# A fused scan and feed-forward kernel: attention operands loaded ahead of the weights, sign rows made in one go, the order searched anew

## The chip, the core and the metric

The kernel runs on one core of a Trainium2 chip. The core has TensorE (PE, matrix multiplies, with weight loads shown apart as PEld), VectorE (DVE), ScalarE (ACT) and GpSimd (POOL), and SyncE (SP), whose queue issues every DMA of this kernel. [...] The metric is the device time of one execution in microseconds, as the median of several runs; less is better.

## The reference, cut to what matters

A chunked linear recurrence with decay produces an array of 3072 tokens by 256, and a feed-forward layer follows:

```
log_a = log(clip(a, 1e-6, 1))
for c in chunks:                          # the chunk length is free
    cum   = cumsum(log_a[chunk])
    M     = (C @ B.T) * exp(cum_i - cum_j) * (i >= j)
    y     = M @ x + (C @ state) * exp(cum_i)
    state = exp(cum_last) * state + sum_j exp(cum_last - cum_j) * outer(B_j, x_j)
h = y @ w_in                              # 3072 x 256 by 256 x 2048
g = h - tanh(h)
out = g @ w_out                           # 2048 x 256
```

There are 4 batches, 8 heads, 768 positions, 32 columns per head and 16 state rows per head. All is float32.

## The kernel before, in words

**Attention part.** Each batch is cut into 7 chunks of 112 positions (the last has 96). The 16 state rows sit as extra rows 0 to 15 beside the 112 positions, so one product per head gives both the inner and the carried part. For a chunk, TensorE makes decay differences (L447 for the first three chunks, L512 for the later ones) and the products of B and C (L458, L521) in the PSUM tile `att`; ScalarE takes the exponential (L465, L536) into `lt`; VectorE multiplies by the products (L470, L540); GpSimd zeroes what is not causal (L475, L543); TensorE makes `y` (L569, L575). ScalarE copies the new state from `y` into the rows of the next chunk's `x` (L580), and `y` is split into a high and a low part, `xh` by ScalarE (L593) and `xl` by VectorE (L598). So each chunk hands its state to the next, and the chunks of a batch form a chain.

**Decays.** `a` arrives in `a_sb`, is clipped on VectorE (`logs`, L804), and ScalarE takes the logarithm into `la` (L840), then loads the table for the exponential (L817). TensorE sums `la` (L863, L868); ScalarE takes the sums as `ncum` (L897) and `rows` (L873); VectorE splits the rows into three bfloat16 `parts` (L877 to L875); a DMA stores them (L882), and small DMAs read them back into rows of `lt_c` (L888) and `rt_c` (L890). L512 multiplies `lt_c` with `rt_c`: the rows that were read back are the sums, the other rows of a group of nine are ones or signs. The ones of `lt_c` come from a GpSimd memset (L827). The signs of `rt_c` are `lt_c` while it is still all ones, times the column `par` (L496): four instructions in two spans of chunks, and the loads into `lt_c` of a span wait for them.

**Feed-forward part.** Tokens are taken in 12 tiles of 256. The two halves of a 256-row piece of the weights come by DMA as `raw` and are split by `conv` (L348 to L372) into `wh` and `wl`. A step (tile, piece) is `mm1` (L646, 12 matmuls), `act` (tanh L661, difference L665, split L669 and L676) and `mm2` (L709, 12 matmuls). Steps (0,0) and (0,1) use unsplit operands (L630, L701).

**Order.** All work is listed as operations with an engine, a cost and dependencies (class `Order`). A table of numbers, `RANK`, gives each a priority; a list scheduler (`schedule`) with the written costs makes a plan, and the operations are issued in the order of that plan. SP allows itself eight transfers in flight. In gaps of TensorE that the plan shows in its first 65 us, `fill` (L434) puts in matmuls whose result is not used; `warm` (L834) does so at the start. The number of fills in a long gap depends on `LATE`.

Of the kernel before, what the change touches and what calls it, by code (L numbers as in the profile page):

```python
# [42 lines left out]
NPH, NL, NSW, NRAW, NGB, LAG, WARM = 2, 3, 4, 2, 3, 2, 8  # L43
SWEEPS = 0, 2, 4, 6, 8
AHEAD = 32
LULL, SPARE, PIECE, LATE = 65.0, 0.35, 0.215, 1.4
# [207 lines left out]
def tile_ssm_moe(ctx: ExitStack, tc: tile.TileContext, a, x, bn, bc, wts, out):  # L254
    nc = tc.nc
# [569 lines left out]
    def ones(i):  # L825
        v = lt_c[:, SPAN[i]].rearrange("p c m -> p (c m)")
        nc.gpsimd.memset(v, 1.0)  # L827
# [175 lines left out]
```

## Time and profile before

| | |
|---|---|
| median of three runs | 336.06 us (334.4 to 338.8) |
| profiled execution | 337.54 us, span 335.8 us |
| TensorE busy | 326.6 us (97%) |
| VectorE busy | 226.6 us (67%) |
| ScalarE busy | 192.0 us (57%) |
| GpSimd busy | 56.8 us (17%) |

The span is from the first to the last instruction that the profile records; 1.7 us of the profiled execution lie around it. Shares over the span are averages over stages with different limits: the first 42 us carry little feed-forward work, the rest carries most of it.

### The profile page before, as it was taken

To read this page: it belongs to the slowest core of one execution; us is meant where nothing else is said; L and a number is where in the kernel's file an instruction comes from. 1 tells how busy PE (TensorE), PEld (TensorE's weight loads), DVE (VectorE), ACT (ScalarE), POOL (GpSimd) and SP (SyncE) were. 2 spreads that over 40 slices of the span, in tenths; PEclk is the share of its full clock that TensorE was granted. 3 is DMA by queue.
4 is the path that set the end of the run, shared out by engine and by line. 5 is a ranking of instruction groups with operands and counts; after the bars stand their busy time and mean duration, and the time that the engine had idled before them with its cause. 6 is when DMAs were issued, how large, how long until landed. Compare 5 with 4: busy or idle time off the path is not lost.

```text
span 335.8 us, 9087 instructions
## 1 busy us (share of the span) xinstructions
PE 326.6 (97%) x3872; PEld 314.4 (94%) x3872; DVE 226.6 (67%) x332; ACT 192.0 (57%) x404; POOL 56.8 (17%) x74
## 2 busy tenths in 40 slices
PE   8899999999999999999999999999999999999995
PEld 6788789999999999999999999999999999999995
DVE  2779999999998975645555655655655655654552
ACT  5766888784775644344555645643656645644441
POOL 6543464610102110000011101101111101100000
PEclk9699999999999999999999999999999999999999
DMA  6939668640102102010011200200200100100000
GB/s 158 263 112 307 153 230 193 194 143 0 48 9 68 32 0 65 31 33 2 31 48 31 64 12 20 64 20 13 62 4 2 33 2 2 33 0 2 31 2 32
DMA packets 12472, 21.41 MB, mean 64 GB/s; under 512 B 2848, under 2 KB 7648, under 8 KB 12432
## 3 DMA queue, kind: packets, MB, share of 16 engines
q1 hardware_dynamic: 12432, 20.84, 21.9%
q8 instruction: 30, 0.49, 0.6%
q14 instruction: 10, 0.08, 0.1%
HBM read 17.51 MB, written 3.32 MB: 62 GB/s over the span
## 4 chain that ended last, share of the span: by engine, by line
PE 87%; DMA 4%; DVE 4%; issue 2%; ACT 1%; POOL 1%; SPq 1%; POOLq 0%
PE o L709 39%; PE ph L646 38%; PE y L569 4%; PE att L521 3%; DMA bc<-bc_d 3%; DMA raw<-w_d 2%; PE att L512 1%; PE cp L447 1%; PE y L575 1%; POOL lt L543 1%; DVE lt L470 1%; DVE wm L353 0%; DVE g L665 0%; PE att L458 0%; DVE rt_c L496 0%
## 5 line engine op out<-in xcount | busy, mean ns | idle before, releaser
L665 DVE TENSOR_TENSOR g<-ph,g 128x512 f32<-128x512 f32 x96 | 66.1, 690 | 55.9 <-ACT g L661 55.9
L661 ACT ACTIVATE g<-ph 128x512 f32<-128x512 f32 x96 | 57.5, 599 | 74.3 <-PE ph L646 71.7
L646 PE MATMUL ph<-xh,wh 128*128 128x256 f32 x376 | 95.3, 278 | 0.2 <-DVE g L665 0.2
L646 PE MATMUL ph<-xh,wl 128*128 128x256 f32 x376 | 94.5, 276 | 0.0
L676 DVE TENSOR_TENSOR gl<-g,gh 128x512 fp32r<-128x512 f32 x94 | 66.7, 713 | 26.6 <-ACT gh L669 24.0
L669 ACT CAST gh<-g 128x512 fp32r<-128x512 f32 x94 | 58.2, 619 | 36.0 <-DVE g L665 29.7
L646 PE MATMUL ph<-xl,wh 128*128 128x256 f32 x376 | 73.2, 276 | 0.0
L646 PEld LDWEIGHTS ph<-xh,wh 128*128 128x128 f32 x376 | 70.6, 188 | 0.8 <-DVE g L665 0.4
L646 PEld LDWEIGHTS ph<-xh,wl 128*128 128x128 f32 x376 | 70.6, 188 | 0.0
L709 PE MATMUL o<-gh,wh 128*128 128x256 f32 x376 | 60.2, 282 | 0.0
L709 PE MATMUL o<-gh,wl 128*128 128x256 f32 x376 | 57.9, 276 | 0.0
L709 PE MATMUL o<-gl,wh 128*128 128x256 f32 x376 | 57.9, 276 | 0.0
L646 PEld LDWEIGHTS ph<-xl,wh 128*128 128x128 f32 x376 | 56.6, 188 | 0.0
L709 PEld LDWEIGHTS o<-gh,wh 128*128 128x128 f32 x376 | 49.8, 188 | 1.1
L709 PEld LDWEIGHTS o<-gh,wl 128*128 128x128 f32 x376 | 49.6, 188 | 0.0
L709 PEld LDWEIGHTS o<-gl,wh 128*128 128x128 f32 x376 | 49.6, 188 | 0.0
L543 POOL TENSOR_SCALAR_AFFINE_SELECT lt<-lt 128x896 f32<-128x896 f32 (+1 forms) x25 | 28.6, 1143 | 122.3 <-DVE lt L540 109.5
L540 DVE TENSOR_TENSOR lt<-att,lt 128x896 f32<-128x896 f32 (+1 forms) x25 | 26.6, 1065 | 2.8 <-ACT lt L536 2.1
L396 POOL TENSOR_TENSOR bw<-braw,wdec 128x256 f32<-128x256 f32 x14 | 12.3, 886 | 90.7 <-PE y L575 89.9
L536 ACT ACTIVATE lt<-att 128x896 f32<-128x896 f32 (+1 forms) x25 | 22.6, 904 | 1.4 <-PE att L521 0.3
L580 ACT COPY x<-y 16x64 f32<-16x64 f32 x96 | 19.4, 202 | 6.4 <-DVE xl L598 3.5
L569 PE MATMUL y<-lt,x 128*32 128x112 f32 (+1 forms) x448 | 16.8, 268 | 1.9 <-POOL lt L543 1.2
(79 smaller groups left out, 264.1 us busy)
## 6 DMA issues: line engine op xcount, KB each, us to landing
raw<-w_d SPq DMA_DIRECT2D x16, 512.0 KB
x<-x_d SPq DMA_DIRECT2D x14, 256.0 KB
bc<-bc_d SPq DMA_DIRECT2D x56, 60.0 KB
out_d<-ob SPq DMA_DIRECT2D x16, 128.0 KB
braw<-bn_d SPq DMA_DIRECT2D x14, 112.0 KB
out_d<-pt SPq DMA_DIRECT2D x8, 128.0 KB
cum<-parts SPq DMA_DIRECT2D x1, 168.0 KB
lt_c<-cum SPq DMA_DIRECT2D x4, 27.0 KB
```

What stands on the lines that cost most here:

```text
L396: nc.gpsimd.tensor_tensor(out=d["b"].rearrange("p c (h n) -> p c h n", h=H), in0=d["braw"].rearrange("p c (h n) -> p c h n", h=H), in1=wd. ...
L536: nc.scalar.activation(k["l"][:, :, 0:q].rearrange("p (i w) q -> p i w q", i=4), place[1][:, :, 0:2, N : N + q], AF.Exp)
L540: nc.vector.tensor_tensor(out=lt, in0=place[1][:, :, 2:4, N : N + q], in1=lt, op=ALU.mult)
L543: nc.gpsimd.affine_select(out=k["l"][:, :, 0:q], in_=k["l"][:, :, 0:q], pattern=[[0, H], [1, q]], compare_op=ALU.is_ge, fill=0.0, base=N, ...
L569: nc.tensor.matmul(out=y[D * h : D * h + D, hg * Q : hg * Q + q], lhsT=d["x"][:, cg, P * hg + D * h : P * hg + D * h + D], rhs=k["l"][:, 4 ...
L580: nc.scalar.copy(grp[(ck + 1) // CPG]["x"][0:N, (ck + 1) % CPG, 2 * D * i : 2 * D * i + 2 * D], k["y"][D * i : D * i + N, H * D : H * D + ...
L646: nc.tensor.matmul(out=ph[:, j, :], lhsT=w_[:, u, 0, k, j * P : (j + 1) * P], rhs=d[("xh", "xl")[p]][:, k, ts], start=p == 0 and k == 0 an ...
L661: nc.scalar.activation(g, gs[t, u][0], AF.Tanh)
L665: nc.vector.tensor_tensor(out=g, in0=ph, in1=g, op=ALU.subtract)
L669: nc.scalar.copy(gh, gs[t, u][1])
L676: on.tensor_tensor(out=gl, in0=g, in1=gh.bitcast(F32), op=ALU.subtract)
L709: nc.tensor.matmul(out=po[t, seg][:, e, :], lhsT=w_[:, u, 1, j, e * P : (e + 1) * P], rhs=g[:, j, :], start=u == seg[0] and k == 0 and j = ...
```

## The change

The sign rows are made early and for all chunks at once: VectorE sets the 3200 columns of one half of `rt_c` to one, and two multiplications by the columns of `par` write the second half and then the first. The four multiplications of before (L496) are gone, and with them the wait of the loads into `lt_c`. `WARM` goes from 8 to 10 and `LATE` from 1.4 to 0.6. The planner counts a longer lag from a DMA to its reader. `RANK` is a new table.

```
-NPH, NL, NSW, NRAW, NGB, LAG, WARM = 2, 3, 4, 2, 3, 2, 8
+NPH, NL, NSW, NRAW, NGB, LAG, WARM = 2, 3, 4, 2, 3, 2, 10
...
-LULL, SPARE, PIECE, LATE = 65.0, 0.35, 0.215, 1.4
+LULL, SPARE, PIECE, LATE = 65.0, 0.35, 0.215, 0.6
...
-147 351 639 203 244 86 296 353 131 427 266 928 811 84 242 227 476 72 88 71 191 74 773 287 117 117 324 209 273 250 172
...
+128 962 150 26 11 291 361 128 296 162 1269 342 704 181 590 195 876 1242 131 302 195 963 256 1239 184 545 130 28 258
...
     def lag(self, a, b):
-        return self.DMA_LATENCY if a == "DMA" else 0.0 if a == b else self.SEM_PE if "PE" in (a, b) else self.SEM
+        if a == "DMA":
+            return {"POOL": 2.4, "DVE": 1.3, "ACT": 1.3}.get(b, self.DMA_LATENCY)
+        return 0.0 if a == b else self.SEM_PE if "PE" in (a, b) else self.SEM
...
                 s = ck // 2
                 sl = SPAN[s]
-                for w in range(2):
-                    op("DVE", (0.45, 0.8)[s], lambda w=w, sl=sl: nc.vector.tensor_scalar(
-                           out=rt_c[:, w, sl], in0=lt_c[:, sl], scalar1=par[:, w : w + 1], scalar2=None, op0=ALU.mult),
-                       r=[l_c[s], "par", k["n_l"][1]], w=[r_c[s]])
...
     r_c = op.pieces("rt_c", 2)
+    sign = [rt_c[:, w, SPAN[0].start :].rearrange("p c m -> p (c m)") for w in range(2)]
+    op("DVE", 0.9, lambda: nc.vector.memset(sign[0], 1.0), w=r_c)
+    for w in (1, 0):
+        op("DVE", 0.95, lambda w=w: nc.vector.tensor_scalar(out=sign[w], in0=sign[0], scalar1=par[:, w : w + 1], scalar2=None,
+                                                            op0=ALU.mult), r=["par"], w=r_c)
```

**VectorE at the start.** The first of the program's rows on VectorE, before (L804 is the clip of `a`, L807 to L813 make `par` and `idn`, L353 begins the first weights):

```order
L789 MEMSET a_sb 16x224
L790 MEMSET a_sb 32x32
L804 TENSOR_SCALAR a_sb<-a_sb 128x224
L807 TENSOR_SCALAR pid<-pid 128x1
L808 TENSOR_SCALAR pid<-pid 128x1
L809 CAST pidf<-pid 128x2
L810 CAST ncf<-ncol 128x16
L811 TENSOR_SCALAR par<-pidf 128x1
L812 TENSOR_SCALAR par<-pidf 128x1
L813 TENSOR_SCALAR idn<-ncf,pidf 128x16
L353 TENSOR_SCALAR wm_163<-raw_126 128x512
L358 TENSOR_SCALAR wv_170<-wv_170 128x512
```

and in the change (L848 and L850 are the new work, L805 is the clip):

```order
L790 MEMSET a_sb 16x224
L791 MEMSET a_sb 32x32
L848 MEMSET rt_c 128x3200
L808 TENSOR_SCALAR pid<-pid 128x1
L809 TENSOR_SCALAR pid<-pid 128x1
L810 CAST pidf<-pid 128x2
L811 CAST ncf<-ncol 128x16
L812 TENSOR_SCALAR par<-pidf 128x1
L813 TENSOR_SCALAR par<-pidf 128x1
L814 TENSOR_SCALAR idn<-ncf,pidf 128x16
L850 TENSOR_SCALAR rt_c<-rt_c,par 128x3200 x2
L805 TENSOR_SCALAR a_sb<-a_sb 128x224
```

The clip moved from third to last of these, behind the memset, the small constants and both sign multiplications; the first two weight instructions moved behind the split of the rows.

**VectorE in the first tile.** Before, around the sign multiplications of the second span (`lt` and `xl` belong to the first three chunks, `wl`, `wm`, `wv` to the first weights):

```order
L470 TENSOR_TENSOR lt_287<-att,lt_287 128x448
L353 TENSOR_SCALAR wm_377<-raw_223 128x1024
L372 TENSOR_TENSOR wl<-wv_170,wh 128x512
L496 TENSOR_SCALAR rt_c<-lt_c,par 128x2304
L598 TENSOR_TENSOR xl_320<-y_331,xh_311 128x2x112
L358 TENSOR_SCALAR wv_388<-wv_388 128x1024
L361 SCALAR_TENSOR_TENSOR wm_377<-wv_388,wm_377 128x1024
```

and the same place in the change:

```order
L475 TENSOR_TENSOR lt_287<-att,lt_287 128x448
L377 TENSOR_TENSOR wl<-wv_221,wh 128x512
L599 TENSOR_TENSOR xl_317<-y_333,xh_302 128x2x112
L358 TENSOR_SCALAR wm_382<-raw_246 128x1024
L377 TENSOR_TENSOR wl<-wv_221,wh 128x512
L363 TENSOR_SCALAR wv_406<-wv_406 128x1024
L366 SCALAR_TENSOR_TENSOR wm_382<-wv_406,wm_382 128x1024
```

The multiplication is gone, and `xl` of the second chunk stands ahead of one `wl` and of `wm`.

**SP at the start.** The first transfers before:

```order
L315 DMA braw_99<-bn_d 112x256
L792 DMA a_sb<-a_d 112x192
L794 DMA a_sb<-a_d 96x32
L325 DMA raw_126<-w_d 128x1024
L294 DMA bc_128<-bc_d 16x960 x4
L325 DMA raw_126<-w_d 128x1024
L306 DMA x_141<-x_d 128x512
L306 DMA x_144<-x_d 128x512
```

and in the change:

```order
L793 DMA a_sb<-a_d 112x192
L299 DMA bc_131<-bc_d 16x960
L795 DMA a_sb<-a_d 96x32
L311 DMA x_134<-x_d 128x512
L299 DMA bc_131<-bc_d 16x960
L311 DMA x_145<-x_d 128x512
L299 DMA bc_131<-bc_d 16x960 x2
L320 DMA braw_99<-bn_d 112x256
L330 DMA raw_153<-w_d 128x1024 x2
```

The attention operands `bc`, `x` and `braw` moved ahead of the first weights `raw`; the second piece of `a` keeps the third place.

## Rows read from the trace of the kernel before

**Rows 1.** The page's engine line: busy time, share of the span, instructions.

```profile
PE 326.6 (97%) x3872; PEld 314.4 (94%) x3872; DVE 226.6 (67%) x332; ACT 192.0 (57%) x404; POOL 56.8 (17%) x74
```

**Rows 2.** Busy time by stretch: stretch, its length, then PE, PEld, DVE, ACT, POOL busy with instructions, granted TensorE clock, DMA share, GB/s.

```profile
7.60:18.70 11.10, 9.02 (x109) 7.95 (x107) 7.07 (x15) 8.72 (x30) 4.28 (x6) 0.69 0.97 253
18.70:42.10 23.40, 21.54 (x344) 18.37 (x343) 22.90 (x30) 16.94 (x41) 10.95 (x12) 1.00 0.66 188
42.10:68.70 26.60, 26.37 (x435) 24.30 (x420) 26.33 (x34) 22.13 (x51) 14.32 (x14) 1.00 0.71 201
...
100.00:331.50 231.50, 231.50 (x2613) 227.31 (x2612) 138.08 (x204) 119.02 (x239) 19.52 (x25) 1.00 0.09 26
```

**Rows 3.** The timeline in order of time (start, duration, engine, line, what; in brackets the idle time before it and what ended it): the first feed-forward step with split weights, and the one later idle gap of TensorE.

```profile
42.14 0.38 PE L646 MATMUL ph<-xh,wh 128*128 128x256 f32 x1
...
68.70 0.38 PE L646 MATMUL ph<-xh,wh 128*128 128x256 f32 x1 [0.23 <-DVE g L665]
```

**Rows 4.** The timeline of the opening: clip, logarithm, tables, constants, and the first exponential.

```profile
1.20 0.09 DVE L790 MEMSET a_sb<- 32x32 f32 x1
...
3.60 0.28 DVE L804 TENSOR_SCALAR a_sb<-a_sb 128x224 f32<-128x224 f32 x1 [2.31 <-DMA a_sb<-a_d]
...
3.90 0.61 ACT L840 ACTIVATE la<-a_sb 128x224 f32<-128x224 f32 x1 [1.61 <-DVE a_sb L804]
3.94 0.15 DVE L807 TENSOR_SCALAR pid<-pid 128x1 int32<-128x1 int32 x1
...
4.53 1.28 ACT L817 ACT_TABLE_LOAD   x1
...
4.64 0.33 DVE L813 TENSOR_SCALAR idn<-ncf,pidf 128x16 f32<-128x16 f32 x1
...
5.83 0.20 ACT L817 ACTIVATE tab<-const-float32-1.0 128x1 f32<-128x1 f32 x1
...
7.60 0.68 ACT L348 ACTIVATE wv<-raw 128x512 f32<-128x512 f32 x1 [1.57 <-DMA raw<-w_d]
...
8.18 0.35 ACT L873 COPY rows<-pr 112x256 f32<-112x256 f32 x1
...
8.43 0.36 ACT L897 ACTIVATE ncum<-pr 128x224 f32<-128x224 f32 x1
8.65 0.29 DVE L877 CAST parts<-rows 112x256 bf16<-112x256 f32 x1
8.82 1.09 ACT L465 ACTIVATE lt<-cp,ncum 128x112 f32<-128x112 f32 x4
```

**Rows 5.** Groups of instructions in the first 90 us, shapes apart: busy time, mean ns of one, idle time before and its releaser.

```profile
L496 DVE TENSOR_SCALAR rt_c<-lt_c,par 128x2304 bf16<-128x2304 bf16 x2 | 2.1, 1066 | 0.0
L496 DVE TENSOR_SCALAR rt_c<-lt_c,par 128x896 bf16<-128x896 bf16 x2 | 1.1, 608 | 0.0
L353 DVE TENSOR_SCALAR wm<-raw 128x512 uint32<-128x512 uint32 x2 | 0.8, 424 | 2.6 <-DMA raw<-w_d 2.6
L358 DVE TENSOR_SCALAR wv<-wv 128x512 f32<-128x512 f32 x2 | 0.8, 422 | 0.3 <-ACT wv L348 0.3
L789 DVE MEMSET a_sb<- 16x224 f32 x1 | 0.2, 245 | 0.9 <-PEq L993 0.9
L827 POOL MEMSET lt_c<- 128x2304 bf16 x1 | 2.0, 2022 | 0.0
L470 DVE TENSOR_TENSOR lt<-att,lt 128x448 f32<-128x448 f32 x6 | 3.7, 622 | 3.6 <-ACT x L580 2.2 <-PE att L458 1.4
```

**Rows 6.** Busy time of VectorE alone in two stretches (length, busy time with instructions, granted clock, DMA share, GB/s); the second ends with the split of the fifth chunk.

```profile
8.65:18.70 10.05, 6.31 (x14) 0.66 0.98 254
18.70:40.90 22.20, 21.70 (x29) 1.00 0.66 189
```

**Rows 7.** The timeline of ScalarE's one long wait between the first exponentials.

```profile
14.31 0.62 ACT L369 CAST wh<-wv 128x512 fp32r<-128x512 f32 x1 [1.64 <-DVE wv L365]
```

**Rows 8.** TensorE's timeline: the warm-up, the sums and first differences, the idle gap, and the same differences later.

```profile
0.84 3.59 PE L834 MATMUL warm<-const-float32-1.0 128*32 128x128 f32 x16 [0.84 <-PEq L993]
...
4.66 0.66 PE L863 MATMUL pr<-upto,la 128*112 128x128 f32 x4 [0.23 <-POOL after L799]
...
5.54 1.04 PE L447 MATMUL cp<-upto,la 128*128 128x112 f32 x8
...
9.55 0.71 PE L458 MATMUL att<-bc 16*128 16x112 f32 x16 [1.70 <-POOL bc L403]
...
12.85 3.75 PE L447 MATMUL cp<-upto,la 128*128 128x112 f32 x16
```

**Rows 9.** The granted clock of TensorE by microsecond (stretch, length, PE busy, granted clock, DMA share, GB/s).

```profile
12.00:13.00 1.00, 1.00 (x17) 0.50 1.14 186
...
18.00:19.00 1.00, 1.00 (x20) 0.95 0.56 160
```

**Rows 10.** The chain of waits that ended last (start, length, what), where a sign multiplication stands on it.

```profile
24.31 1.11 DVE rt_c L496
```

**Rows 11.** SP's issues of the first weights and of the store of the parts in the timeline, and TensorE's first use of what is read back.

```profile
2.18 0.43 SPq L325 DMA_DIRECT2D raw<-w_d  x1
...
10.21 0.33 SPq L882 DMA_DIRECT2D cum<-parts  x1
...
27.03 0.27 PE L512 MATMUL att<-rt_c,lt_c 9*128 9x224 bf16 x4
```

97 rows, old and new, of the table RANK are left out of this document.

## The prediction

> **What bounds the kernel now.** The page's engine line comes first: TensorE is busy 97% of the span [rows 1]. Shares over the span hide stages, so the stretches come next [rows 2]. From 42.1 us on TensorE hardly rests: 26.37 of 26.60 us, and from 100 on 231.50 of 231.50. The first step with split weights starts at 42.14, and the only later gap of note is 0.23 us at 68.70 [rows 3]. The blocks of TensorE after that step are the same in number in both kernels. So whatever the change gains or loses ahead of that step moves the end by as much, provided that the engines which feed TensorE keep up. The question is what sets 42.14.
>
> Between 18.70 and 42.10 VectorE is busy 22.90 of 23.40 us [rows 2], while most of what TensorE then does is short or filler. Up to the split of the fifth chunk, at 40.90, which stands just ahead of the step, VectorE's busy time is 6.31 us from 8.65 to 18.70 and 21.70 us from there [rows 6]: 28.01 us of work and 4.24 us of waiting. VectorE's queue is the account in which I make the sum. Its first entry, at 8.65, is the split of the sums of `la`, just before the first exponential at 8.82 [rows 4].
>
> **The change, part by part.**
>
> *Sign multiplications removed.* Two of 1066 ns and two of 608 ns [rows 5]: 3.35 us, all within the account. One of them is a link of the chain that ended last, with 1.11 us [rows 10].
>
> *Memset added on VectorE.* It has 3200 bfloat16 columns, and no row shows such a memset on VectorE. The nearest in engine and operation is the float32 one of 224 columns in 245 ns [rows 5], 1.09 ns a column: 3.5 us. GpSimd's bfloat16 memset, 2304 columns in 2022 ns, gives 2.8 us. VectorE's own bfloat16 multiplication, 2304 columns in 1066 ns, gives 1.5 us, the lower end. I take 3.5, since engine and operation are the same, and keep 1.5 for the range.
>
> The type is what these rows leave open. The Trainium skill, page "VectorE: DVE Perf Modes", section "Zero memsets can be issued as uint32 (trn2)", says that a memset takes one cycle per element whatever the dtype. At that page's 0.96 GHz this would be an estimate of 3.3 us, and the sum below would be 0.2 us better. Before, no run shows a bfloat16 memset on VectorE.
>
> *Two sign multiplications added.* 3200 columns at the rate of the 2304 ones: 1.48 us each, 2.96 together.
>
> *The clip moves behind all this.* The small memsets end at 1.29 and the seven constants take 1.03 us, from 3.94 to 4.97 [rows 4]; in the change GpSimd makes their sources first, so they don't wait. The clip then ends at 1.29 + 3.50 + 1.03 + 2.96 + 0.28 = 9.06, instead of 3.88. Behind it on VectorE is all else, and ScalarE waits for it: logarithm 0.61, then table load and its use 1.50 (4.53 to 6.03), so 11.2.
>
> *ScalarE's wait for the weights goes.* Before, ScalarE stood 1.57 us until 7.60 for the first weights and converted them before the sums, so the late clip costs less than its 5.2 us. In the change `ncum` and `rows` come first, 0.36 and 0.35 us [rows 4]: the rows are there at 11.9, and VectorE's account starts there, 3.25 us later than at 8.65. If the sums on TensorE run at half rate, they end later than 11.2 and it is 12.3.
>
> *Weight instructions moved into the account.* The first `wm` and `wv`, 424 and 422 ns [rows 5], stood before 8.65: +0.85.
>
> *Waiting within the account.* 4.24 us before. ScalarE stood 1.64 us between the first exponentials for a `wv` of VectorE [rows 7]; in the change the conversions to `wh` come after all six groups of exponentials, so I take 1.64 off: 2.6 remain. Ends: 0.6 if the 3.6 us that VectorE waited ahead of its first `lt` multiplications all go [rows 5], and 4.24 if none.
>
> *The sum.* 11.9 + (28.01 - 3.35 + 0.85) + 2.6 = 40.0, against 40.90: a gain of 0.9 us. With the ends of the waiting and of the start, 11.9 + 25.5 + 0.6 = 38.0 (2.9 gained) and 12.3 + 25.5 + 4.24 = 42.0 (1.1 lost).
>
> *What costs nothing.* **Transfers:** the weights are issued tenth instead of fourth. They took 5.4 us from issue to use (2.18 to 7.60) [rows 4, 11], and the two `x` and four `bc` now ahead of them, 0.77 MB by their shapes, at 253 GB/s [rows 2] take 3 us more: about 11 us. They are wanted after the first two groups of exponentials (1.09 us each) and so after 14; without that cover ScalarE's queue would stop and the exponentials behind. The parts are stored 3 us later than at 10.21, and what is read back is first used 16.8 us after the store, at 27.03 [rows 11]; the reads no longer wait for VectorE. **Warm-up:** four more matmul instructions at 3.59/16 us [rows 8] are 0.9 us, done before 6, long before the sums can start at 9.7. Fewer fills leave TensorE idle where it has nothing to do. The longer lags are numbers of the planner and no instructions. **After 42 us:** one chunk's attention stands later among the steps, the same work for TensorE. VectorE is nearly as full as TensorE there, 26.33 of 26.60 us, so a gain is passed on only as VectorE is early too, and here it is VectorE that is early. What is late next is VectorE's difference at 68.70.
>
> The profiled execution of 337.54 us becomes 336.6. It is 1.48 us over the median of the runs, so the forecast for a median is 336.06 - 0.9 = **335.2 us**.
>
> **The rivals.**
>
> *A fast memset.* If it runs like the bfloat16 multiplications, in 1.5 us, everything up to the first exponential is 2.0 us earlier: 333.2 us. For it: VectorE's bfloat16 multiplications are over twice as fast per column as its float32 memset. Against it: that memset, and GpSimd's bfloat16 one, at 0.88 ns a column. The page's sentence above speaks against it too. Chance 0.2.
>
> *Slower: the opening is a chain, not a queue.* The first exponential needs the first differences. From the sums to those is 1.92 us (4.66 to 6.58) at the higher clock [rows 8]. Before, the granted clock was 1.00 there. It was 0.50 by 12 to 13 us, back by 18 to 19 [rows 9], after TensorE had idled 1.70 us before 9.55 [rows 8]. At that level sixteen of the differences take 3.75 us instead of 2.08, 1.8 times as long. In the change TensorE idles from the warm-up's end until 9.7, over 4 us; at 1.2 GHz the differences are ready at 9.7 + 3.5 = 13.2, and the first exponential is 4.4 us late. If the chunks then follow one another through ScalarE, VectorE, GpSimd and TensorE with no slack, only the multiplications on that chain come back, 1.11 us [rows 10] and one of 1.07: 4.4 - 2.2 = 2.2 us lost, 338.3 us. It decides from the point at which VectorE waits more than 40.9 - 11.9 - 25.5 = 3.5 us within the account. For it: part of the waiting ahead of `lt` was for such a chain, 2.2 us for ScalarE's state copies [rows 5]. Against it: VectorE had 0.5 us of idle time after 18.7. Chance 0.2.
>
> *Nothing comes through.* The start is as late as the removed work is long, 3.25 against 3.35, and the waiting stays: 42.0 to 42.2 either way, 336 us. Chance 0.15.
>
> **How the numbers follow.** The forecast's case has 0.45: 335.2, from 333.2 to 337.2 with its ends. Ranged with the others, and with the 2 us by which single runs of the kernel before stand off their median, 332.0 to 337.8 should hold it 8 times in 10; outside lie the fast memset with little waiting and the chain at its full loss. Two per cent, 6.7 us, is about what a measurement of this kernel tells from no change: 329.3 and 342.8. Faster would need the fast memset and all waiting gone at once (2.0 + 2.9 = 4.9 is still short), 0.04; slower more than twice the chain's loss, 0.02; within, 0.94.
>
> **What would show it.** The duration of the one memset on `rt_c` (3.5 or 1.5); the end of the clip (9.1); the first exponential (12, 13 if the clock is low, 10 if the memset is fast); VectorE's waiting up to the fifth chunk's split (2.6); and the first step with split weights, at 41.2 instead of 42.14. After it TensorE should have no gap over some 0.3 us. The prediction is wrong if that step moves as forecast and the end does not, or if ScalarE waits for the first weights again.

## The result and the profile after

The changed kernel takes 338.24 us (median of 20 runs, 337.26 to 338.63), the kernel before 336.26 us (20 runs, 334.11 to 338.80): ratio 1.0057, 95% interval 1.0034 to 1.0081. It is about 2 us slower where 0.9 us of gain was forecast. The profiled execution is 338.18 us, span 336.5. Two single executions far outside all others, one of 1123 us with the clip first and one of 363 us of the kernel before, are left out of the ratios below.

The engine line of the changed kernel's page answers to [rows 1]:

```profile
PE 325.0 (97%) x3864; PEld 312.6 (93%) x3864; DVE 227.6 (68%) x331; ACT 191.0 (57%) x404; POOL 54.6 (16%) x74
```

The opening in its timeline (start, duration, engine, line, what; in brackets the idle time before and what ended it), VectorE and ScalarE, beside [rows 4]:

```profile
2.01 2.73 DVE L848 MEMSET rt_c<- 128x3200 bf16 x1 [0.73 <-issue]
4.65 0.10 DVE L808 TENSOR_SCALAR pid<-pid 128x1 int32<-128x1 int32 x1
...
5.32 2.15 DVE L850 TENSOR_SCALAR rt_c<-rt_c,par 128x3200 bf16<-128x3200 bf16 x2
7.38 0.47 DVE L805 TENSOR_SCALAR a_sb<-a_sb 128x224 f32<-128x224 f32 x1
...
11.23 0.29 DVE L883 CAST parts<-rows 112x256 bf16<-112x256 f32 x1 [3.39 <-ACT rows L879]
...
15.14 0.62 DVE L475 TENSOR_TENSOR lt<-att,lt 128x448 f32<-128x448 f32 x1 [2.03 <-ACT lt L470]
16.86 0.62 DVE L475 TENSOR_TENSOR lt<-att,lt 128x448 f32<-128x448 f32 x1 [1.09 <-PE att L463]
```

```profile
12.32 1.09 ACT L470 ACTIVATE lt<-cp,ncum 128x112 f32<-128x112 f32 x4 [1.12 <-PE cp L452]
```

TensorE's timeline there, beside [rows 8], and by microsecond its busy time and granted clock (stretch, length, busy with instructions, clock, DMA share, GB/s), beside [rows 9]:

```profile
8.63 1.17 PE L869 MATMUL pr<-upto,la 128*112 128x128 f32 x4 [4.07 <-ACT la L841]
9.59 0.95 PE L874 MATMUL pr<-la,upto 128*128 128x224 f32 x2
10.34 3.59 PE L452 MATMUL cp<-upto,la 128*128 128x112 f32 x16
...
16.66 2.04 PE L452 MATMUL cp<-upto,la 128*128 128x112 f32 x16
```

```profile
8.00:9.00 1.00, 0.37 (x2) 0.50 1.00 315
13.00:14.00 1.00, 1.00 (x6) 0.56 0.50 138
14.00:15.00 1.00, 1.00 (x19) 1.00 1.15 187
```

The clip ends at 7.85 instead of 3.88, TensorE idles 4.07 us, and then everything up to the first sixteen differences runs at the lower of its two levels: 3.59 us for what takes 2.04 a little later. The first exponential is at 12.32, 3.5 us late.

VectorE's account, from the split of the rows to the start of the fifth chunk's `xl`, beside [rows 6] (busy time of VectorE alone); then the first step with split weights and TensorE behind it, beside [rows 2, 3]:

```profile
11.23:41.89 30.66, 26.09 (x38) 0.96 0.69 184
```

```profile
43.51 0.39 PE L647 MATMUL ph<-xh,wh 128*128 128x256 f32 x1
```

```profile
43.50:70.00 26.50, 26.50 (x436) 24.65 (x425) 26.21 (x35) 22.52 (x53) 11.78 (x15) 1.00 0.76 216
```

The account begins 2.58 us later than at 8.65 and lasts 30.66 us instead of 31.87 (8.65 to 40.52): 26.09 busy, 4.57 waiting. So the step comes 1.37 us later than at 42.14. Behind it TensorE has no gap any more, and 0.60 us come back: the last matmul ends at 332.57 instead of 331.80.

That is 0.77 us between the two profiles and 2 us between the medians, because the profiled run of before was one of its long ones. Single runs of before differ by up to 4.7 us, those of the change by 1.4, and the mean granted clock that each run lists says which is which: of 31 runs of before in the first series below, 16 were at 0.997 or more and took 333.8 to 335.7 us, 15 at 0.983 to 0.993 and took 335.8 to 338.6. In all four series below the runs of before at 0.997 or more, 64 in all, have a median of 334.4 to 334.6, so medians of different series can be set side by side, and the change is 3.7 us above a kernel before that stays at the upper level. In the changed kernel the clock says much less: its two runs at 1.000 took 337.8 and 338.0, and all 20 lie within those 1.4 us.

### The profile page after: what moved, and what is told of

Its sections match the earlier page's. It is cut to its first block, busy times and chain, and to the rows that moved or that the text cites. A ratio compares the mean times of both kernels' runs of the same rounds, so it can differ in the third digit from the quotient of the medians.

```text
span 336.5 us, 9065 instructions
## 1 busy us (share of the span) xinstructions
PE 325.0 (97%) x3864; PEld 312.6 (93%) x3864; DVE 227.6 (68%) x331; ACT 191.0 (57%) x404; POOL 54.6 (16%) x74
## 4 chain that ended last, share of the span: by engine, by line
PE 89%; DVE 4%; issue 2%; ACT 2%; SPq 1%; DMA 1%; POOL 1%; POOLq 0%; DVEq 0%
PE o L710 39%; PE ph L647 38%; PE y L570 4%; PE att L522 3%; PE cp L452 1%; PE att L513 1%; DMA braw<-bn_d 1%; POOL lt L544 1%; DVE wm L366 1%; PE y L576 1%; DVE lt L541 1%; DVE wl L377 1%; SPq L299 1%; DVE wv L363 0%; PE att L463 0%
## 5 line engine op out<-in xcount | busy, mean ns | idle before, releaser
L677 DVE TENSOR_TENSOR gl<-g,gh 128x512 fp32r<-128x512 f32 x94 | 65.9, 704 | 26.0 <-ACT gh L670 23.4
L544 POOL TENSOR_SCALAR_AFFINE_SELECT lt<-lt 128x896 f32<-128x896 f32 (+1 forms) x25 | 26.8, 1072 | 167.0 <-DVE lt L541 154.2
```

What stands on the lines that cost most here:

```text
L544: nc.gpsimd.affine_select(out=k["l"][:, :, 0:q], in_=k["l"][:, :, 0:q], pattern=[[0, H], [1, q]], compare_op=ALU.is_ge, fill=0.0, base=N, ...
L677: on.tensor_tensor(out=gl, in0=g, in1=gh.bitcast(F32), op=ALU.subtract)
```

## The experiments

Two theories were set against each other. **Queue:** the opening is VectorE's list of work, taken in the order of issue (in the change the clip starts at 7.38 us, behind both multiplications, while in the kernel before its data was there at 3.60), so time is its start plus its work plus a waiting that can be told beforehand (the forecast). **Chain:** the chunks follow one another through ScalarE, VectorE, GpSimd and TensorE, so time is the start plus TensorE's rate, and VectorE's work counts only where a link waits for it. This table has, from one profiled run of each, the first exponential, the start and end of VectorE's account as above, its busy and waiting time, the end of the last matmul, and the median of the runs (us).

| kernel | first exp. | start | end | busy | waiting | last matmul | median |
|---|---|---|---|---|---|---|---|
| before (profiled) | 8.82 | 8.65 | 40.52 | 27.63 | 4.24 | 331.80 | 336.26 |
| changed | 12.32 | 11.23 | 41.89 | 26.09 | 4.57 | 332.57 | 338.24 |
| before again | 8.22 | 8.04 | 40.03 | 27.63 | 4.36 | 331.33 | 335.17 |
| clip first | 7.86 | 10.47 | 40.47 | 26.55 | 3.45 | 331.25 | 336.07 |
| long warm-up | 10.80 | 10.55 | 39.50 | 26.10 | 2.85 | 330.19 | 335.98 |
| no memset | 9.55 | 8.46 | 38.76 | 26.11 | 4.19 | 329.74 | 335.61 |
| before, signs early | 8.30 | 8.13 | 37.09 | 25.07 | 3.89 | 328.90 | 335.48 |
| before, filled | 8.22 | 8.04 | 37.06 | 27.65 | 1.37 | 328.34 | 334.54 |
| before, both | 8.69 | 7.99 | 39.26 | 25.22 | 6.05 | 331.10 | 334.50 |
| weights first | 7.88 | 7.77 | 38.01 | 26.27 | 3.97 | 328.70 | 334.70 |
| both, fewer fills | 8.36 | 8.18 | 36.53 | 25.33 | 3.02 | 328.45 | 334.21 |
| filled, fewer fills | 7.82 | 7.64 | 37.31 | 27.67 | 2.00 | 329.16 | 335.19 |
| weights first, filled | 7.88 | 7.77 | 38.01 | 26.10 | 4.14 | 328.70 | 334.56 |
| before, signs as changed | 12.34 | 11.01 | 41.36 | 25.19 | 5.16 | 332.66 | 338.82 |

### The kernel before again

No edit. 

> The kernel before the change, unchanged, for a second trace and for the spans and clocks of its single runs, which spread from 334.1 to 338.8 us. If the spread comes from the granted clock in the opening, single runs with a clock of 1.00 have spans about 3 us shorter than those with 0.989, and a trace of a short one shows no half-rate stretch between 11 and 18 us. If it comes from elsewhere, spans and clocks don't go together.

Median 335.17 us, ratio 0.9991 (0.9954 to 1.0027). Its three runs at a clock of 0.989 or 0.990 took 337.1 to 337.8 us, its seven at 0.997 or more 334.1 to 335.8. The profiled one is of the first kind; TensorE's timeline and granted clock:

```profile
6.84 1.04 PE L447 MATMUL cp<-upto,la 128*128 128x112 f32 x8
8.94 0.71 PE L458 MATMUL att<-bc 16*128 16x112 f32 x16 [1.06 <-POOL bc L403]
9.58 1.14 PE L447 MATMUL cp<-upto,la 128*128 128x112 f32 x8
11.10 1.21 PE L458 MATMUL att<-bc 16*128 16x112 f32 x16 [0.38 <-DVE lt L470]
12.24 3.75 PE L447 MATMUL cp<-upto,la 128*128 128x112 f32 x16
```

```profile
10.00:11.00 1.00, 0.73 (x7) 0.97 1.20 143
11.00:12.00 1.00, 0.90 (x16) 0.50 1.11 176
15.00:16.00 1.00, 1.00 (x9) 0.50 0.97 269
16.00:18.00 2.00, 2.00 (x48) 0.56 0.77 215
```

The engine idles 1.06 us, works on, and from 11 to 17 us is at 0.50. The baseline itself pays for the clock, in some of its runs.

### The clip first

The change, with the memset and both sign multiplications issued behind the clip; all other queues as in the change.

```
+        at = max(order.index(i) for i in self.behind)
+        order = [i for i in order[: at + 1] if i not in self.moved] + self.moved + order[at + 1 :]
```

> The changed kernel with one thing moved: on VectorE the memset and the two sign multiplications come behind the clip of a instead of ahead of it; nothing else changes place. Theory late clip (the loss comes from the clip that ends at 7.85 instead of 3.88 us): the clip ends at about 4, the first exponential is at about 9 instead of 12.3, the first step with split weights at about 41 instead of 43.5, and the time falls by 2 to 3 us to about 335.5. Theory clock (the half-rate stretch from 7.5 to 13.5 us is what costs): the stretch moves or stays and the time falls only if it goes. Theory queue (VectorE's work alone sets the step): the split of the rows waits until the signs end at about 9.2, so the step moves by under 2 us, time about 336.5.

Median 336.07 us, ratio 1.0016 (0.9979 to 1.0053): about 2.2 us of the change's loss come back. The first exponential is at 7.86, but now the rows' split waits for the sign work (10.47), TensorE waits 2.61 us for the first multiplication of `lt`, and its next sixteen differences take 3.75 us. Two runs whose clock read 1.00 took 335.1 and 335.2.

### A long warm-up

The change with 27 warm-up instructions instead of 10, so that TensorE works up to the late sums; nothing else differs.

```
-NPH, NL, NSW, NRAW, NGB, LAG, WARM = 2, 3, 4, 2, 3, 2, 10
+NPH, NL, NSW, NRAW, NGB, LAG, WARM = 2, 3, 4, 2, 3, 2, 27
```

> The changed kernel with a warm-up of 27 instead of 10 matmuls in the program, so that TensorE is busy until the logarithm is there; the plan and every other instruction stay. Theory clock: no half-rate stretch around 8 to 13 us, the first exponential at about 11.3 instead of 12.3 and the first multiplication of lt at 14 instead of 15.1, the first step with split weights about 1 us earlier than 43.5, time about 337.2. Theory late clip: the clip stays at 7.85 and the step moves by less than 0.4 us, time 338.

Median 335.98 us, ratio 1.0007 (0.9976 to 1.0037), every run at 0.997 or more and within 0.8 us of the others. The clip is as late as in the change (logarithm at 7.89), yet 2.3 us come back: that is what the lower rate cost. The differences start at 9.67 instead of 10.34 and take 1.93 us instead of 3.59, VectorE waits 0.34 us instead of 2.03 for the first multiplication of `lt`, and the account's waiting falls from 4.57 to 2.85. VectorE's timeline, then busy time by engine over the account (PE, PEld, DVE, ACT, POOL) and granted clock:

```profile
12.78 0.62 DVE L475 TENSOR_TENSOR lt<-att,lt 128x448 f32<-128x448 f32 x1 [0.34 <-PE att L463]
```

```profile
10.55:39.50 28.95, 27.02 (x415) 22.52 (x414) 26.10 (x38) 23.13 (x68) 13.04 (x15) 1.00 0.73 198
```

### No memset

The change, with the sign rows made from the ones that GpSimd writes for `lt_c`, and behind the clip.

```
-    op("DVE", 0.9, lambda: nc.vector.memset(sign[0], 1.0), w=r_c)
+    one_s = lt_c[:, SPAN[0].start :].rearrange("p c m -> p (c m)")
...
-out=sign[w], in0=sign[0]
+out=sign[w], in0=one_s
```

> The changed kernel without the memset on VectorE: both sign halves are made by multiplying the ones of lt_c, which GpSimd makes anyway, and stand behind the clip. Theory late clip: clip at about 4, signs from about 5 to 7.2, the rows are split at about 8, the first step with split weights at 40 to 41, time 334 to 335.5, less than in the run with the clip first. Theory queue: VectorE has 3.35 us less work than before the change and an earlier start, so the same. Theory clock: no gain unless the half-rate stretch goes.

Median 335.61 us, ratio 0.9992 (0.9964 to 1.002). Its start is nearly that of before (8.46), its granted clock reads 1.00 throughout, 3.35 us of sign work are out of the account, and it is no faster than before. Its first sixteen differences still took 2.90 us, after 0.58 us of idling ahead of the sums. VectorE's timeline shows two more delays:

```profile
3.67 1.40 DVE L807 TENSOR_SCALAR a_sb<-a_sb 128x224 f32<-128x224 f32 x1 [1.46 <-DMA a_sb<-a_d]
...
11.87 0.43 DVE L360 TENSOR_SCALAR wm<-raw 128x512 uint32<-128x512 uint32 x1 [1.87 <-DMA raw<-w_d]
12.21 0.62 DVE L477 TENSOR_TENSOR lt<-att,lt 128x448 f32<-128x448 f32 x1
```

The clip takes 1.40 us beside GpSimd's memset, and VectorE stands 1.87 us for the first weights, with the first multiplication of `lt` behind: the later transfers, hidden in the change by its late start (its `wm` at 12.69 waits for nothing), are not hidden once the start is early.

### Before, sign rows early

One part alone: the kernel before, with two multiplications of 3200 columns from `lt_c`'s ones where VectorE idled for the first weights, and the four later ones gone.

```
-    op("DVE", (0.45, 0.8)[s], lambda w=w, sl=sl: nc.vector.tensor_scalar(
-           out=rt_c[:, w, sl], in0=lt_c[:, sl], scalar1=par[:, w : w + 1], ...
+    if s == 0:
+        op.moved.append(len(op.ops))
+    op("DVE", (0.45, 0.8)[s], None if s else lambda w=w: nc.vector.tensor_scalar(
+           out=sign[w], in0=one_s, scalar1=par[:, w : w + 1], ...
```

> The kernel before, with the sign rows alone changed: two multiplications of 3200 columns, from the ones that GpSimd has already written for the other operand, stand behind the constants on VectorE, where it idles 2.4 us for the first weights; the four later ones are gone, and there is no memset. All other queues are as before. Theory of the queue (the account of the prediction): VectorE loses 3.35 us within the account and the start does not move, so the time falls by about 3 us, to some 332.8. Theory of the chain: only the two multiplications that stood between steps that wait for one another come back, 1.1 to 2.2 us, so 333.5 to 334.6. If the time is that of before (335.7), neither VectorE's work nor its place mattered here. In each case the single runs should go on spreading over some 4 us with the granted clock, as those of before do.

Median 335.48 us, ratio 1.0002 (0.9966 to 1.0039): nothing, and the spread with the clock stays (333.7 to 338.5). Its eight runs at 0.997 or more have a median of 334.7, no better than before's at that clock. Both expectations fell, the chain's too.

### Before, TensorE filled

The kernel before, with four fills where TensorE idles 1.06 us.

```
+            if i == self.keep:
+                self.fill(4, None)
```

> The kernel before, with one thing added: four idle matmul instructions (about 0.9 us) behind the second group of differences, where TensorE idles 1.06 us and after which its granted clock falls to 0.50 in the profiled runs. If the spread of the single runs before (333.8 to 338.6) is the clock, every run is at a mean clock of 0.997 or more and at 333.8 to 335.8, median 334.5. If it is not the clock, or the idle stretch is not what lowers it, the runs spread as before around 335.7.

Median 334.54 us, all twelve runs at 0.998 or more and between 334.0 and 335.0; ratio 0.9984 (0.9965 to 1.0003). The spread of the kernel before was the clock, and four unused matmul instructions take it away. VectorE alone over the account in its two profiled runs, first this one, then the one before it:

```profile
8.04:37.06 29.02, 27.65 (x41) 1.00 0.83 225
```

```profile
8.13:37.09 28.96, 25.07 (x37) 1.00 0.75 218
```

In both the granted clock reads 1.00 throughout. The sign work is 2.58 us of busy time less, the waiting 2.52 us more (3.89 against 1.37), and the end is the same. In the timeline of the run with the early signs 1.36 of those 2.52 us stand ahead of two later `xl`, for state copies of ScalarE, and 0.51 more ahead of a `wv`, which waits 0.17 us in the filled kernel:

```profile
25.74 0.39 DVE L602 TENSOR_TENSOR xl<-y,xh 128x224 fp32r<-128x224 f32 x1 [0.98 <-ACT x L584]
...
31.19 0.39 DVE L602 TENSOR_TENSOR xl<-y,xh 128x224 fp32r<-128x224 f32 x1 [0.38 <-ACT x L584]
...
33.09 0.69 DVE L360 TENSOR_SCALAR wv<-wv 128x1024 f32<-128x1024 f32 x1 [0.68 <-ACT wv L350]
```

### Both together

> Both edits together on the kernel before: sign rows early without a memset, and TensorE filled over its idle stretch. Theory of the chain: 334.5 less 1.1 to 2.2, so 332.3 to 333.4, with little spread. Theory of the queue: about 331.5. If the two edits give the same microseconds twice, as the late clip and the clock seem to do in the changed kernel, it is no better than the better of the two alone.

Median 334.50 us, ratio 0.998 (0.9952 to 1.0008): no better than the fills alone. Its profiled run is the one of twelve at 336.84; its differences ran slowly (1.89 us for eight) after 0.56 us of idling ahead of the sums.

### Weights first, in the change without memset

```
+        order.remove(self.first)
+        order.insert(order.index(self.second) + 1, self.first)
```

> The changed kernel without its memset (as in the earlier run), and in addition the first half of the first weights is issued fourth on SyncE's queue again, as in the kernel before, ahead of the first operands of attention. In the run without the memset VectorE stands 1.87 us for these weights, with the first multiplication of attention behind. If that wait is on the path, the first such multiplication is up to 1.3 us earlier and the time is about 334.5; if the path runs through the differences and attention, nothing comes of it (335.6), and if the first operands of attention, now 2 us later, are what is missing, it is 336 or more.

Median 334.70 us, ratio 0.9985 (0.9963 to 1.0008), 0.9 us below the run without it. The first multiplication of `lt` moves from 12.21 to 10.78. How much of this is the order of the transfers isn't shown, since the two profiled runs also differ in their sums' rate (0.66 us for the first four here, 1.16 there).

### Fewer fills

In the filled kernel before, nine of the 22 fills ahead of the third chunk's outputs are taken out, and one warm-up instruction is added; once with the sign rows early, once without.

```
+ - 9 * (lull[i] > 3.0)
```

> The kernel before with the sign rows early (no memset) and TensorE filled over its idle stretch, as in the run with both edits, and two edits more: one warm-up instruction more, so that TensorE does not idle ahead of the sums, and nine of the 22 fills taken out that stand on TensorE's queue ahead of the third chunk's outputs. Where the sign rows alone were moved, VectorE's saved work came back as waiting, 0.98 us of it before the third chunk's split, and those outputs began only when 4.8 us of fills had ended, at 22.80, 2.4 us after their attention was ready. If the fills are that wait, the third chunk's split is 1 us earlier than 25.74 and the time some 0.7 to 1 us below 334.5: 333.6. If something else ends the wait (GpSimd's decayed operands, done at 22.4 for both groups), the time stays at 334.5.

> The same without the sign rows: the kernel before, TensorE filled over its idle stretch, one warm-up instruction more, and the nine fills taken out. Here VectorE was busy 27.65 of 29.02 us and hardly waited for the third chunk's outputs, so taking the fills out alone should give nothing: 334.5, as with the filled idle stretch alone. If it gains as much as the run with the sign rows, the sign rows are worth nothing even when the way is free for them, and the fills were the loss.

With the sign rows 334.21 us, ratio 0.9969 (0.994 to 0.9998); without them 335.19, ratio 1.0006 (0.9985 to 1.0027). Only with them is the third chunk's split earlier, 25.20 instead of 25.74 (25.96 without them, in a run whose first sums were slow). So the freed VectorE time is worth half a microsecond once TensorE's queue is not filled ahead of the outputs; the account ends 0.53 us earlier than with the fills alone. But the last matmul does not (328.45 against 328.34): it is lost again behind the first split step, at places not looked into, and the 0.3 us between the medians is within their spread. This is the fastest version tried, 0.3% below before, hardly clear of its interval.

### Weights first, filled

Four fills, here behind the last sums, and one more warm-up instruction in the change without memset, weights first.

> The changed kernel without its memset, sign rows behind the clip, first half of the first weights issued fourth, as in the earlier run, and now TensorE filled where it idled in that run: one warm-up instruction more and four fills behind the last sums, 0.86 us, after which its granted clock fell to 0.50 from 12.6 to 15.5. If that was all that the run still lost, every run is at 0.997 or more; by what the low stretch cost there (3.66 instead of 2.04 us for sixteen differences) the time of the profiled kind falls by some 1.5 us to 332.5 to 333.2. If the first differences are as slow as in the runs in which TensorE had idled ahead of the sums, nothing comes of it: 334.5.

Median 334.56 us, ratio 0.9971 (0.9942 to 1.0001); all runs at 0.997 or more. The gain foreseen did not come: the sixteen differences take 2.04 us instead of 3.66, but the account ends at 38.01 in both. Part was paid at once, since the fills moved the first multiplication of `lt` from 10.78 to 11.27. The rest is lost ahead of the first chunk's split, which starts at 17.59 and 17.57: with the fills VectorE has no gap from 12.99 up to it, so there its own queue is the limit.

### Before, with the change's sign rows and nothing else

Memset, constants and both multiplications ahead of the clip; order, transfers and fills of before.

```
+    parts_s = [lambda: nc.vector.memset(sign[0], 1.0), lambda: times(1), lambda: times(0), None]
...
+        order = [i for i in order[:at] if i not in self.moved] + self.moved + ...
```

> The kernel before with the sign rows done exactly as in the change, and nothing else of it: memset of 3200 columns, constants and two sign multiplications ahead of the clip on VectorE, the four later multiplications gone; the order of all other work, the transfers, the lags' plan and the fills are those of before. Theory of the chain: the clip ends near 8 as in the changed kernel, TensorE idles some 4 us ahead of the sums, the first differences run at half rate, and none of the removed multiplications comes back, since moving them alone gave nothing: 334.5 of an undisturbed run of before, plus 2.5 for the start, plus about 2 for the rate, so 338 to 339, and the new order and transfers of the change are worth little or nothing. Theory of the queue (the prediction's account): start 3.2 us later, VectorE's work 3.35 us less, so about 335. If it is above 339.5, the new order of the change had earned back part of what its sign rows cost.

Median 338.82 us, ratio 1.0116 (1.0079 to 1.0153). The sign rows as the change makes them, ahead of the clip, are enough for the whole loss: 4.3 us against the filled kernel before. Its first differences are slow, and here the clock column does not say so (TensorE's timeline, then busy time and granted clock):

```profile
8.65 1.17 PE L875 MATMUL pr<-upto,la 128*112 128x128 f32 x4 [4.21 <-ACT la L845]
...
10.36 1.89 PE L449 MATMUL cp<-upto,la 128*128 128x112 f32 x8
...
12.77 1.04 PE L449 MATMUL cp<-upto,la 128*128 128x112 f32 x8
```

```profile
10.00:11.00 1.00, 1.00 (x6) 1.00 0.85 96
11.00:12.00 1.00, 1.00 (x6) 1.00 0.16 23
```

## Why the prediction was wrong, point by point

**What bounds.** That a shift ahead of the first split step reaches the end was right, but for the 0.60 us won back behind it. That VectorE's queue alone sets the step was wrong. Removing 2.58 us of its work left the end where it was, since the waiting rose by as much: the path through the other engines was just as long. That VectorE was nearly full because work for it had been placed where it would have waited is a reading, not shown.

**The late clip.** Its terms were too high but for the clip. From the end of the small memsets at 1.29 to the next instruction at 4.65 the memset takes 3.36 us, against 3.5: its row has 2.73 us, and 0.73 of idle time stand ahead of it for which the profile names no releaser ("issue"). The Trainium skill, page "VectorE: DVE Perf Modes", section "Zero memsets can be issued as uint32 (trn2)", had given an estimate of 3.3 us (one cycle per element whatever the dtype); this bfloat16 memset of ones agrees with it if that idle time is counted in, and its row alone is shorter. The constants took 0.75 us against 1.03, the two sign multiplications 2.07 against 2.96 (the two of 2304 columns from which they were scaled took 0.94 and 1.19 us, more per column than these), and the clip adds 0.38 against 0.28. So it ended at 7.85, not 9.06. The rows' split began at 11.23, not 11.9, although the sums ran at the lower rate.

**The waiting, the step that failed.** "I take 1.64 off: 2.6 remain" measured 4.57. ScalarE's wait for that `wv` did go, but VectorE now stood 2.03 us for the late first exponential and 1.09 for the next products. The forecast treated waiting as a quantity of the queue. Of before's 4.24 us, 2.87 were the clock: in the filled kernel, same orders, it is 1.37. And the change keeps the clock loss rather than shedding it: with the long warm-up, its waiting is 2.85, and its account ends at 39.50 + 0.38 = 39.9, where the forecast said 40.0. That the two ends agree is in part luck, because a start 1.35 us too late made up for about 1 us of busy time and 0.25 of waiting that were missing. But the sum is nearly the one of a change whose TensorE does not slow down, set against a kernel before that had already slowed down; against an undisturbed before (37.06 + 0.38 = 37.4) it would be a loss of 2.6 us.

**From the profile to the median, a second step that failed.** The forecast took the profiled 336.6 and went 1.48 us down, because the profiled run of before lay that far above its median. That offset was before's mix of clock levels, and the change does not have it: its profiled run is 0.06 us below its median. So about half of the 3.0 us by which the median missed come from this step, and half from the account and what came back behind it.

**Busy time.** 25.5 was forecast up to the split's end, 26.09 + 0.38 measured: about 1 us more. The change's first `wl` of 1024 columns took 1.92 us (32.01 to 33.93) while GpSimd made a product (32.82 to 34.43), against 1.21 before; the rest of the excess is not traced.

**What was costed at nothing.** The weights arrived in time, as said, but only because the start was late; with an early start VectorE stood 1.87 us for them. The later gap of 0.23 us at 68.70 went away. TensorE's idling up to the late sums, over 4 us, stood in the sum only as an end of the range, 12.3 for 11.9; filling it gave back 2.3 us.

**The rivals.** The second, "a chain, not a queue", has the mechanism that the runs bear out: VectorE waited 4.57 us, beyond its point of 3.5. Its place was right too: the first exponential at 12.32 after differences at the lower level (13.2 was foreseen). One part of it was not: it gave back 2.2 us for the removed multiplications, and moving them alone gave nothing. That its 338.3 us lie beside the measured 338.24 is therefore luck: in the profiles the step is 1.37 us late where this rival said 2.2, and the median adds what the mix of clock levels hid. It had a chance of 0.2 and should have had the largest: the same profile had the low clock after 1.70 us of idling [rows 8, 9], and the change made that idling over 4 us. The third, "nothing comes through", is nearest in the account: 42.0 to 42.2 foreseen, 41.89 + 0.38 = 42.27 measured, with a start 2.58 us late instead of 3.25. Its 336 us failed at the same step from the profile to the median, and its waiting stayed near 4.24 only as a sum, by other waits than before's. The fast memset fell. That the time stays within 2% was right.

**What stays open.** How the 3.7 us between the changed and the filled kernel before divide is known only roughly, 2.3 for the rate by the long warm-up and the rest for the start. The shares overlap, since each cure alone gives back 2.2 to 2.6 us, and two of those are more than 3.7. The new order's own worth was not measured apart from the late clip; against the run with the sign rows alone it is 0.6 us in its favour by the medians, and 2 us by the ratios, whose medians of before (334.62 and 336.26) differ in how many runs were at the low clock, so that the first is the fairer. With the sign rows out of the clip's way the changed order, weights first and filled, takes 334.56 us, where the filled order of before takes 334.54: no worth of the new order shows there.

## What to carry to other kernels

Work put into an idle stretch of one engine is not free if the first instruction of a chain stands behind it; look first at which instruction of that queue the other engines wait for. When taking work off an engine that looks full, find what its next wait would be, because the waiting may grow by the same amount. When single runs of a baseline spread, sort them by their granted clock before forecasting against the median: here four unused matmul instructions were worth about as much as any other edit.

## What the runs showed of the hardware

**The rate without the clock column.** After 4.21 us of idling TensorE's matmuls ran 1.8 times as long (1.89 against 1.04 us for eight differences) while the granted clock stood at 1.00; in the changed kernel a slowing of the same size is recorded as 0.50. The Trainium skill, page "TensorE: Matmul & The Clock Gate", section "Part 1: The HAM clock gate (the "warmup" mystery)", warns that the clock gate's trace events are unreliable on trn2. These rows fit that warning but do not show that it was the clock; the durations are the better witness of the rate.

Half a microsecond of idling ahead of the sums does not decide it. The first four sums, from the runs without memset, with the clip first, and filled with fewer fills (no idling ahead), all while the granted clock read 1.00:

```profile
5.86 1.16 PE L872 MATMUL pr<-upto,la 128*112 128x128 f32 x4 [0.58 <-ACT la L843]
```

```profile
5.84 0.66 PE L872 MATMUL pr<-upto,la 128*112 128x128 f32 x4 [0.56 <-POOL braw L825]
```

```profile
4.79 1.20 PE L867 MATMUL pr<-upto,la 128*112 128x128 f32 x4
```

What decides it stays open.

**GpSimd beside VectorE.** GpSimd's three small copies into `braw` took 1.07 us together in the kernel before and 2.63 us beside the sign multiplications of the change:

```profile
5.03 1.07 POOL L822 COPY braw<-idn 16x256 f32<-16x256 f32 x3
```

```profile
5.47 2.63 POOL L823 COPY braw<-idn 16x256 f32<-16x256 f32 x3 [0.58 <-DVE idn L814]
```

The other way round, in the run without memset on VectorE, the clip took 1.40 us beside GpSimd's memset of `lt_c`, against 0.28 before.
